# Attention with a soft mixture of experts: the second layer and the outputs in four pieces of 128 columns, with two batches to an output tile

## Chip, core and metric

One core of one Trainium2 chip (trn2). The metric is device time in microseconds (us) of one execution. TensorE is PE in the profile (PEld its weight loads), VectorE DVE, ScalarE ACT, GpSimd POOL; SP is the queue from which all transfers named here are issued. L922 is line 922 of the kernel before. In the changed kernel the same operations have other line numbers, given where they are needed.

## What is computed

```python
q_rot, k_rot = rotate(q), rotate(k)              # 8 batches, 8 heads, 576 tokens, 64 columns
attn = softmax(q_rot @ k_rot.T / sqrt(64)) ; x = attn @ v      # x: 4608 tokens x 512
logits = x @ phi                                 # 4608 x 32: 8 experts with 4 slots each
d = softmax of logits over the tokens ; slot_input = d.T @ x   # 32 x 512
for e in range(8):
    h = max(slot_input[e] @ w1[e], 0)            # 4 x 1024, w1[e]: 512 x 1024
    slot_out[e] = h @ w2[e]                      # 4 x 512,  w2[e]: 1024 x 512
c = softmax of logits over the slots
out = c @ slot_out                               # 4608 x 512
```

All inputs and outputs are float32.

## The kernel before

The attention takes some 420 us of the span and is the same in both kernels. The change lies in the last 65 us, and in one place at 424 us.

**Last pair of heads.** `natural_last` (L430) transposes the last pair's result on PE, nine transposes of 64 columns into two PSUM banks: five from the upper 64 rows, then four from the lower 64. ACT copies the first bank (L439), DVE the second (L440). `logits_add` (L454) then uses them.

**First layer.** `ffn1_steps` multiplies 32-column stationary blocks (the slots) by the 32 weight tiles of w1, 512 columns at a time (L899). DVE applies the maximum with zero (L904), `ffn1_turn` transposes the result on PE (L911) and ACT copies it to `hts` (L912).

**Weights.** w1 and w2 come in 64 tiles of 512 KB (`load_w`, L632), all issued from SP. The tiles of w2 for the output columns 0 to 255 (`mh` = 0) come first, then those for the columns 256 to 511 (`mh` = 1). The pool `wp` has 28 buffers named `w_exp`; weight tiles, small intermediate tiles and output tiles all go through it.

**Second layer.** `ffn2_steps(mh, so)` has 16 steps. A step is four matmuls with 32 stationary columns each, side by side in the four column blocks of the array, and 256 moving columns of a w2 tile (L922). Each float32 matmul shows as two rows in the trace, so a step is 8 rows. After step 15 ACT copies the sum (L926) and DVE takes the remainder (L927); `gather` adds both over the experts with two float32r matmuls (L933), and ACT copies the result to `dn` or `sl` (L936).

**Output.** `combine(mh, sl, b)` makes one output tile of 128 x 1024: for each of two blocks of 128 output columns, a matmul over 512 tokens of batch `b` (L944), a copy from PSUM by ACT for the first block and by DVE for the second (L946), and one transfer of 512 KB (L947). Batch number 8 (`crt`) stands for the 64 last tokens of all batches together. There are 9 tiles for each `mh`, 18 in all.

**Turned combine weights.** The matmul at L944 needs the softmax over the slots, transposed to `cst[q]`, one tile for two batches, and `crt`. `c_split` (L564, L565) splits it into two float32r parts, `c_tr` (L578) transposes them on PE, and copies move them out of PSUM: `c_evac` (L589, L592) in whole width, or `c_evac_late` (L602, L604) per batch, ACT for the first batch of the pair and DVE for the second. So `combine` of batch 4 needs ACT's copies of `q` = 2, batch 5 those of DVE, and batches 6 and 7 those of `q` = 3.

**Order.** PE, ACT and DVE run in the order in which the code is written. Before, `c_turn(2)` stands ahead of the second layer (L975). All 16 steps of `mh` = 0 follow, with one step of `mh` = 1 behind them, then `gather`, `c_tr(3)`, and the table `GROUPS` interleaves the nine combines of `mh` = 0 with the other 15 steps: a number is a batch, a negative number that many steps. The late copies of `q` = 3 come behind the combines of batches 1 and 2. The nine combines of `mh` = 1 end the program:

```python
LEAD_STEPS = 1
GROUPS = ((0, 1, -3), (2, 3, -4), (4, 5, 6, -8), (7, "gather", 8))
```

PSUM: `ps_c` has six banks for `gather`, `c_tr` and `combine`.

Of the kernel before, what the change touches and what calls it, by code (L numbers as in the profile page):

```python
# [19 lines left out]
DM = H * D  # L20
E, SPE, FF = 8, 4, 1024
# [6 lines left out]
N_W = 28  # L28
# [121 lines left out]
def attn_softmoe(ctx, tc, qk, v, phi, w1, w2, cs, ident, sel, seg, out):  # L150
    nc = tc.nc
    P = 128

    const = ctx.enter_context(tc.tile_pool(name="const", bufs=1))
    small = ctx.enter_context(tc.tile_pool(name="small", bufs=3))
    wp = ctx.enter_context(tc.tile_pool(name="wp", bufs=N_W))
# [3 lines left out]
    late = vals.enter_context(tc.tile_pool(name="late", bufs=2))  # L160
# [215 lines left out]
    xns = {}  # L376
# [53 lines left out]
    def natural_last():  # L430
        p = NPAIR - 1
        pp = p % NP
        xts[p] = xt = late.tile([P, S], F32, name="xt", bufs=N_X)
        ts = [bank2(1), bank2(3)]
        for h, cols in enumerate((slice(0, 320), slice(320, S))):
            t = ts[h][:, 0]
            for j in range(5 - h):
                nc.tensor.transpose(t[:, 64 * j:64 * j + 64], xns[B - 1][rows[h], j, pp * P:pp * P + P], id_sb[rows[h], rows[h]])
        nc.scalar.copy(out=xt[:, 0:320], in_=ts[0][:, 0, 0:320])  # L439
        nc.vector.tensor_copy(out=xt[:, 320:S], in_=ts[1][:, 0, 0:256])  # L440
        for t in ts:
            free(t)

# [295 lines left out]
    for t, cc in ((1, 0), (1, 1), (0, 0), (0, 1)):  # L739
        c = half[cc]  # L740
# [39 lines left out]
    seg_in, seg_sb, hts = release_att()  # L780
# [39 lines left out]
    m, al, dt, xn = state["m"], state["al"], state["dt"], xns.pop(B - 1)  # L820
# [26 lines left out]
    for c in range(2):  # L847
        for j in range(4):
            nc.tensor.matmul(sh[c][32 * j:32 * j + 32], lhsT=dn[:, 32 * j:32 * j + 32],
                             rhs=xn[:, j, 256 * c:256 * c + 256], start=True, stop=True, tile_position=(0, 32 * j))  # L850
    for i in range(NP):
        nc.tensor.matmul(rp[32 * i:32 * i + 32], lhsT=dn[0:64, P + 32 * i:P + 32 * i + 32],
                         rhs=xn[0:64, 4, i * P:(i + 1) * P], start=True, stop=True, tile_position=(0, 32 * i))
# [6 lines left out]
                            in1=e.unsqueeze(1).broadcast_to([P, NP, NS]), op=ALU.mult)  # L860
# [24 lines left out]
    for _ in range(N_LEAD):  # L885
# [22 lines left out]
    def ffn1_turn(f, hs):  # L908
        t = ps_t.tile([P, 512], F32, name="t_ps")
        for i in range(4):  # L910
            nc.tensor.transpose(t[:, i * P:(i + 1) * P], hs[:, i * P:(i + 1) * P], id_sb)  # L911
        nc.scalar.copy(out=hts[:, 192 * f:192 * f + 192].rearrange("p (b g k) -> p b g k", g=3, k=SPE)[:, :, 0:3:2],  # L912
                       in_=t.rearrange("p (b g k) -> p b g k", g=8, k=SPE)[:, :, 0:2])

    def ffn2_steps(mh, so):
        op = ps_a.tile([P, 512], F32, name="o_ps")
        og = op[:, 0:256]
        for k in range(16):
            fh, grp, f = k // 8, k // 4 % 2, k % 4
            for x in range(4):  # L920
                at = 192 * fh + 12 * (4 * f + x) + SPE * grp
                nc.tensor.matmul(og[32 * x:32 * x + 32, :], lhsT=hts[:, at:at + 32],  # L922
                                 rhs=w_tiles[4 * E + 16 * mh + 8 * fh + 4 * grp + x][:, f, :],
                                 start=(k == 0), stop=(k == 15), tile_position=(0, 32 * x))
            if k == 15:
                nc.scalar.copy(out=so[:, 0, 0, :], in_=og)  # L926
                nc.vector.tensor_tensor(out=so[:, 1, 0, :], in0=og, in1=so[:, 0, 0, :], op=ALU.subtract)  # L927
            yield

    def gather(mh, so):  # L930
        rp = ps_t.tile([P, 512], F32, name="c_ps")
# [7 lines left out]
    def combine(mh, sl, b):
        ob = wp.tile([P, 4, 256], F32, name="w_exp", bufs=N_W)  # L940
        for jj in range(2):
            o = ps_t.tile([P, 512], F32, name="c_ps")
            tokens = cst[b // 2][:, b % 2] if b < B else crt
            nc.tensor.matmul(o, lhsT=sl[:, P * jj:P * jj + P], rhs=tokens.rearrange("p j i -> p (j i)"), start=True, stop=True)  # L944
            ob2 = ob.rearrange("p j m -> p (j m)")
            (nc.vector.tensor_copy if jj else nc.scalar.copy)(out=ob2[:, 512 * jj:512 * jj + 512], in_=o)  # L946
        nc.sync.dma_start(out=out[mh, b], in_=ob2)  # L947

    turned, split = 2, 3

    def c_turns(n):
        nonlocal turned, split
        for _ in range(n):
            if turned < NP:
                c_turn(turned)
                turned += 1
            if split < min(turned + N_CS, NP):
                c_split(split)
                split += 1
# [17 lines left out]
    steps = ffn2_steps(0, sos[0])
    for k in range(16):
        next(steps)
        if k == 1:  # L980
            ffn1_turn(1, hs)
        if k == 8:
            inner.close()
            ps_s = None
            ps_t = ctx.enter_context(tc.tile_pool(name="ps_c", bufs=6, space=PSUM, reuse_waits="tile"))
    steps = ffn2_steps(1, sos[1])
    for _ in range(LEAD_STEPS):
        next(steps)
    sl0 = gather(0, sos[0])
    c_tr(turned)  # L990
    late_evac = c_evac_late(turned)
    for run_of in GROUPS:
        for b in run_of:
            if isinstance(b, str):
                sl1 = gather(1, sos[1])
            elif b < 0:
                for _ in range(-b):
                    next(steps, None)
            else:
                combine(0, sl0, b)  # L1000
                if b:
                    next(late_evac, None)
    for b in range(B + 1):
        combine(1, sl1, b)


# [50 lines left out]
```

## Time and profile before

| | us |
|---|---|
| median of 3 runs (490.79 to 492.67) | 491.97 |
| the profiled execution | 489.32 |
| its span, on which all times below lie | 487.5 |
| PE busy in the span | 455.4 |
| DVE, ACT, POOL busy | 371.7, 291.1, 288.3 |

The granted TensorE clock was 0.981 of full speed over the span, full from early on until 475 us. The profiled execution is 2.65 us below the median of the runs, and 1.8 us of it lie outside the span. The page's first part gives the busy shares; for this change the last 65 us matter, and there the stretches of the DMA engines are read beside the order of PE.

### The profile page before, as it was taken

What the parts mean: (1) busy time and instruction counts of PE and PEld (TensorE: products, weight loads), DVE (VectorE), ACT (ScalarE), POOL (GpSimd) and SP (SyncE); (2) the same over time, 40 slices, a digit from 0 to 9 for tenths busy, and PEclk for the clock granted to TensorE, in tenths of its full rate; (3) what the DMA queues carried; (4) which work ended last, traced back from release to release, by engine and by line L of the source; (5) the groups of instructions that cost most, each with busy time, mean ns of one, the idle gap of its engine ahead of it and who ended that gap; (6) DMA issues with size and microseconds to landing.
All of it is one profiled execution on the core that took longest, in us unless ns stands there. A gap on an engine that the chain in (4) does not pass through costs nothing.

```text
span 487.5 us, 23593 instructions
## 1 busy us (share of the span) xinstructions
PE 455.4 (93%) x10473; PEld 369.0 (76%) x10473; DVE 371.7 (76%) x626; ACT 291.1 (60%) x668; POOL 288.3 (59%) x320
## 2 busy tenths in 40 slices
PE   4499999999989999999999999999999999899990
PEld 2277788878878888878887888788889888844750
DVE  4999988787868897988898889888977854244370
ACT  2156766775766577657765776567657756542360
POOL 2887759909782969487948795878669102230000
PEclk9699999999999999999999999999999999999996
DMA  7258545563554355435544553354460344989887
GB/s 271 101 186 293 189 134 200 170 229 130 199 170 171 144 182 188 167 110 203 185 156 129 195 190 137 104 209 138 165 216 15 112 161 161 335 289 400 325 342 311
DMA packets 29509, 93.98 MB, mean 193 GB/s; under 512 B 5088, under 2 KB 6880, under 8 KB 29408
## 3 DMA queue, kind: packets, MB, share of 16 engines
q1 hardware_dynamic: 29388, 92.48, 53.0%
q8 instruction: 82, 1.34, 1.1%
q14 instruction: 19, 0.16, 0.1%
q10 hardware_dynamic: 20, 0.00, 0.0%
HBM read 82.95 MB, written 9.44 MB: 190 GB/s over the span
## 4 chain that ended last, share of the span: by engine, by line
PE 84%; DVE 5%; DMA 3%; ACT 2%; issue 2%; POOL 1%; SPq 1%; DVEq 0%; ACTq 0%; POOLq 0%
PE s_ps L356 32%; PE s_ps L321 25%; PE s_ps L268 7%; PE s_ps L336 3%; PE o_ps L922 3%; PE o_ps L899 3%; PE s_ps L465 2%; DMA x_in<-in_qk 2%; PE s_ps L428 2%; DVE nm L270 2%; POOL x_in L220 1%; PE s_ps L277 1%; PE s_ps L525 1%; PE c_ps L944 1%; DVE hl L233 1%
## 5 line engine op out<-in xcount | busy, mean ns | idle before, releaser
L220 POOL TENSOR_TENSOR x_in<-x_in,cs_sb 128x288 f32<-128x288 f32 x248 | 233.0, 975 | 86.5 <-DMA x_in<-in_qk 68.5
L270 DVE TENSOR_REDUCE nm<-s_ps 128x2 f32<-128x576 f32 x256 | 187.9, 752 | 53.6 <-PE s_ps L268 51.9
L322 ACT ACTIVATE a_t<-s_ps 128x576 f32<-128x576 f32 x256 | 145.9, 657 | 7.4 <-PE s_ps L321 7.3
L356 PEld LDWEIGHTS s_ps<-v_in,a_t 128*64 128x64 f32 x4608 | 138.9, 137 | 11.9 <-issue 4.4
L356 PE MATMUL s_ps<-v_in,a_t 128*64 128x66 f32 x4608 | 145.1, 222 | 1.1 <-issue 0.9
L321 PE MATMUL s_ps<-hl 64*128 64x288 f16 x1536 | 133.5, 283 | 1.0 <-DVE nm L270 0.7
L321 PEld LDWEIGHTS <-hl 64*128 64x128 f16 x1536 | 79.5, 94 | 19.9 <-issue 9.8
L321 PE MATMUL s_ps<-peak,lift 64*128 64x288 f16 x512 | 75.3, 282 | 0.5 <-issue 0.5
L268 PE MATMUL s_ps<-hl 64*128 64x288 f16 x512 | 66.4, 287 | 7.1 <-DVE nm L270 3.5
L386 ACT COPY o_sb<-s_ps 128x528 f32<-128x528 f32 x31 | 18.6, 601 | 76.2 <-PE s_ps L356 69.9
L404 POOL TENSOR_TENSOR xn<-o_sb,rr 128x640 f32<-128x640 f32 x31 | 41.1, 1333 | 31.1 <-PE s_ps L525 14.2
L229 ACT CAST hl<-x_in 128x576 f16<-128x576 f32 (+1 forms) x66 | 41.0, 656 | 25.0 <-DVE x_in L224 24.4
L233 DVE TENSOR_TENSOR hl<-x_in,hl 128x1152 f16<-128x1152 f32 x32 | 52.8, 1651 | 2.0 <-ACT hl L229 2.0
L224 DVE TENSOR_TENSOR x_in<-x_in 128x1152 f32<-128x1152 f32 (+2 forms) x36 | 48.3, 1344 | 1.0 <-POOL x_in L220 0.7
L268 PEld LDWEIGHTS <-hl 64*128 64x128 f16 x512 | 30.0, 94 | 22.4 <-issue 11.2
L321 PEld LDWEIGHTS <-lift 64*128 64x128 f16 x512 | 27.1, 94 | 5.0 <-issue 0.7
L356 PE MATMUL s_ps<-v_in,a_tr 64*64 64x66 f32 x1152 | 26.0, 224 | 0.0
L356 PEld LDWEIGHTS s_ps<-v_in,a_tr 64*64 64x64 f32 x1152 | 21.5, 133 | 4.9 <-issue 4.2
L279 DVE TENSOR_REDUCE nm<-s_ps 128x2 f32<-128x576 f32 x32 | 23.9, 749 | 1.0 <-PE s_ps L277 0.8
L336 PE MATMUL s_ps<-hl 64*64 64x320 f16 (+1 forms) x384 | 22.9, 287 | 0.5 <-DVE nm L270 0.3
L340 ACT ACTIVATE a_tr<-s_ps 128x512 f32<-128x512 f32 x32 | 19.1, 597 | 1.1 <-PE s_ps L336 0.4
L448 ACT COPY xt<-s_ps 128x576 f32<-128x576 f32 x31 | 19.0, 652 | 0.0
(170 smaller groups left out, 399.9 us busy)
## 6 DMA issues: line engine op xcount, KB each, us to landing
x_in<-in_qk SPq DMA_DIRECT2D x62, 576.0 KB
w_exp<-in_w SPq DMA_DIRECT2D x55, 512.0 KB
v_in<-in_v SPq DMA_DIRECT2D x32, 330.0 KB
out<-w_exp SPq DMA_DIRECT2D x18, 512.0 KB
wt<-in_w SPq DMA_DIRECT2D x9, 512.0 KB
peak<-mr SPq DMA_DIRECT2D x126, 0.5 KB
x_in<-in_qk SPq DMA_DIRECT2D x4, 288.0 KB
cs_sb<-in_cs SPq DMA_DIRECT2D x2, 288.0 KB
```

The source lines that it names most:

```text
L220: eng.tensor_tensor(out=x[:, :, c], in0=x[:, :, c], in1=cs_sb[:, :, c], op=ALU.mult)
L224: nc.vector.tensor_tensor(out=x[:, t, 0, c], in0=x[:, t, 0, c], in1=x[:, t, 1, c], op=ALU.add)
L229: nc.scalar.copy(out=halves[p][:, 1 + t, c], in_=loaded[p][:, t, 0, c])
L233: nc.vector.tensor_tensor(out=hl[:, 0:4:3], in0=x[:, :, 0], in1=hl[:, 1:3], op=ALU.subtract)
L268: nc.tensor.matmul(s[c, h, 0:HC], lhsT=hl[rows[h], QH, P * j + c.start:P * j + c.stop], rhs=hl[rows[h], KH, half[n]], start=True, stop=True)
L270: nc.vector.tensor_reduce(out=nm[:, n, j:8:4], in_=s[:, :, 0:HC], axis=AX.X, op=ALU.max, negate=True)
L279: nc.vector.tensor_reduce(out=nm[:, :, 8], in_=s[:, :, 0:HC], axis=AX.X, op=ALU.max, negate=True)
L321: nc.tensor.matmul(s[c, h, 0:HC], lhsT=lhs, rhs=rhs, start=(x == 0), stop=(x == 3))
L322: nc.scalar.activation(out=ats[p, b][:, :, half[n]], in_=s[:, :, 0:HC], func=AF.Exp, scale=SCALE)
L336: nc.tensor.matmul(s[rows[h ^ n], n, 0:w] if n else s[rows[h], 0, 512 - w:512], lhsT=lhs, rhs=rhs, start=(x == 0), stop=(x == 3))
L356: nc.tensor.matmul(o[rows[c], h, VW * u:VW * u + VW], lhsT=lhs, rhs=v, start=(i == 0 and u == 0), stop=(left_av[p] == 0 and u == 3 + (c == ...
L404: eng.tensor_tensor(out=xn, in0=t[:, :, :, 0:64], in1=rr.unsqueeze(3).broadcast_to([P, 2, 5, 64]), op=ALU.mult)
```

## The change

- The second layer has four passes (`p` = 0 to 3) of 16 steps with 128 moving columns instead of two with 256. Both passes of an `mh` use the same weight tiles, each half of the columns.
- `gather` and the copies around it run once for each pass, with 128 columns.
- `combine(p, b)` makes one block of 128 output columns for one batch: one matmul, one copy (ACT where `b + p` is even, else DVE). Two neighbouring batches share an output tile and one transfer of 512 KB. The rest (batch 8) is written in four transfers of 256 KB. There are 20 output transfers with the same bytes as 18 before.
- `c_turn(2)` ahead of the second layer is gone; `c_split(3)` stands there. `c_tr(2)` follows the 16 steps of piece 0, and both late turns (`q` = 2 and 3) lie between the combines of piece 0.
- `PIECES` gives the order: `(p, n)` is n steps of pass p, a number is a combine of the current piece, "g1" the gather of pass 1, "c2" `c_tr(2)`, and "e2" one half of the late copies of `q` = 2 (first ACT's, then DVE's).
- `natural_last` issues its nine transposes in turn between the two halves, and DVE's copy stands ahead of ACT's.
- The layout of the output array changes with it.

```diff
-LEAD_STEPS = 1
-GROUPS = ((0, 1, -3), (2, 3, -4), (4, 5, 6, -8), (7, "gather", 8))
+PIECES = (
+    ((0, 16), "c2", (1, 2), "g0", (1, 2), 0, 1, "e2", 2, 3, "e2", "c3", 4, 5, "e3", (1, 1), "e3", 6, 7, 8),
+    ((1, 11), (2, 3), "g1", (2, 2), 0, 1, 2, 3, 4, 5, 6, 7, 8),
+    ((2, 11), (3, 3), "g2", (3, 2), 0, 1, 2, 3, 4, 5),
+    ((3, 11), 6, "g3", 7, 8),
+    (0, 1, 2, 3, 4, 5, 6, 7, 8),
+)
...
-        for h, cols in enumerate((slice(0, 320), slice(320, S))):
-            t = ts[h][:, 0]
-            for j in range(5 - h):
-                nc.tensor.transpose(t[:, 64 * j:64 * j + 64], xns[B - 1][rows[h], j, pp * P:pp * P + P], id_sb[rows[h], rows[h]])
+        for j in range(5):
+            for h in range(2 if j < 4 else 1):
+                nc.tensor.transpose(ts[h][:, 0, 64 * j:64 * j + 64], xns[B - 1][rows[h], j, pp * P:pp * P + P],
+                                    id_sb[rows[h], rows[h]])
+        nc.vector.tensor_copy(out=xt[:, 320:S], in_=ts[1][:, 0, 0:256])
         nc.scalar.copy(out=xt[:, 0:320], in_=ts[0][:, 0, 0:320])
-        nc.vector.tensor_copy(out=xt[:, 320:S], in_=ts[1][:, 0, 0:256])
...
-    def ffn2_steps(mh, so):
+    def ffn2_steps(p, so):
         op = ps_a.tile([P, 512], F32, name="o_ps")
-        og = op[:, 0:256]
+        og = op[:, 0:P]
+        mh, cols = p // 2, slice(P * (p % 2), P * (p % 2) + P)
...
-                                 rhs=w_tiles[4 * E + 16 * mh + 8 * fh + 4 * grp + x][:, f, :],
+                                 rhs=w_tiles[4 * E + 16 * mh + 8 * fh + 4 * grp + x][:, f, cols],
...
+    def combine(p, b):
+        key, half_of = ((p, b // 2), b % 2) if b < B else (("rest", p // 2), p % 2)
+        if key not in obs:
+            obs[key] = wp.tile([P, 4, 256], F32, name="w_exp", bufs=N_W).rearrange("p j m -> p (j m)")
+        ob = obs[key][:, 512 * half_of:512 * half_of + 512]
+        o = ps_t.tile([P, 512], F32, name="c_ps")
+        tokens = cst[b // 2][:, b % 2] if b < B else crt
+        nc.tensor.matmul(o, lhsT=sls["p", p], rhs=tokens.rearrange("p j i -> p (j i)"), start=True, stop=True)
+        (nc.vector.tensor_copy if (b + p) % 2 else nc.scalar.copy)(out=ob, in_=o)
+        if b == B:
+            nc.sync.dma_start(out=out[16 + p // 2][:, 512 * half_of:512 * half_of + 512], in_=ob)
+        elif half_of:
+            nc.sync.dma_start(out=out[4 * p + b // 2], in_=obs.pop(key))
...
-    c_turns(1)
-    sos = [wp.tile([P, 2, 2, 256], F32R, name="w_exp", bufs=N_W) for _ in range(2)]
+    c_split(3)
+    sos = wp.tile([P, 4, 2, P], F32R, name="w_exp", bufs=N_W)
```

How the instructions move is shown at two places. The first is ACT from the sum of the first pass (`w_exp<-o_ps`) on. Before (L946 is the output copy, L602 and L604 the late copies of a turn):

```order
L926 CAST w_exp<-o_ps 128x256
L936 CAST dn<-c_ps 128x256
L946 COPY w_exp<-c_ps 128x512 x2
L602 CAST w_exp<-c_ps 64x2x128 x2
L604 CAST crt<-c_ps 64x64
L602 CAST w_exp<-c_ps 64x2x128 x2
L604 CAST crt<-c_ps 64x64
L946 COPY w_exp<-c_ps 128x512 x5
```

And in the changed kernel (L959 is the output copy, L607 and L609 the late copies):

```order
L932 CAST w_exp<-o_ps 128x128
L947 CAST dn<-c_ps 128x128
L959 COPY w_exp<-c_ps 128x512
L607 CAST w_exp<-c_ps 64x2x128 x2
L609 CAST crt<-c_ps 64x64
L607 CAST w_exp<-c_ps 64x2x128 x2
L609 CAST crt<-c_ps 64x64
L959 COPY w_exp<-c_ps 128x512 x2
L607 CAST w_exp<-c_ps 64x2x128 x2
L609 CAST crt<-c_ps 64x64
L607 CAST w_exp<-c_ps 64x2x128 x2
L609 CAST crt<-c_ps 64x64
```

Two groups of late copies stand among the first output copies instead of one. DVE has the same pattern, one group behind two output copies and the other behind one more.

The second place is PE from the first combines to the end. Before (L922 a step's matmul, four to a step; L944 combine, L933 gather):

```order
L944 MATMUL c_ps<-w_exp,dn 128x512 x4
L922 MATMUL o_ps<-w_exp,hts 32x256 x12
L944 MATMUL c_ps<-w_exp,dn 128x512 x4
L922 MATMUL o_ps<-w_exp,hts 32x256 x16
L944 MATMUL c_ps<-w_exp,dn 128x512 x6
L922 MATMUL o_ps<-w_exp,hts 32x256 x32
L944 MATMUL c_ps<-w_exp,dn 128x512 x2
L933 MATMUL c_ps<-w_exp,seg_sb 128x256 x2
L944 MATMUL c_ps<-crt,dn 128x512 x2
L944 MATMUL c_ps<-w_exp,sl 128x512 x16
```

In the changed kernel, from the last 12 matmuls of the steps ahead of the second gather (L928 a step's matmul, L958 combine, L941 gather):

```order
L928 MATMUL o_ps<-w_exp,hts 32x128 x12
L941 MATMUL c_ps<-w_exp,seg_sb 128x128 x2
L928 MATMUL o_ps<-w_exp,hts 32x128 x8
L958 MATMUL c_ps<-w_exp,dn 128x512 x8
L958 MATMUL c_ps<-crt,dn 128x512
L928 MATMUL o_ps<-w_exp,hts 32x128 x56
L941 MATMUL c_ps<-w_exp,seg_sb 128x128 x2
L928 MATMUL o_ps<-w_exp,hts 32x128 x8
L958 MATMUL c_ps<-w_exp,sl 128x512 x6
L928 MATMUL o_ps<-w_exp,hts 32x128 x44
```

Between the combines of one piece and those of the next now lie 16 steps (or 11) of the narrower form, with a gather among them.

## Rows read from the trace of the kernel before

**Rows 1.** Stretches: busy us (instructions) by engine, TensorE clock, DMA share, GB/s.

```profile
441.00:456.00 15.00, 14.87 (x197) 9.45 (x189) 4.29 (x11) 3.21 (x9) 0.87 (x1) 1.00 1.02 411
456.00:459.40 3.40, 3.39 (x36) 2.12 (x35) 1.43 (x3) 2.17 (x6) 0.00 (x0) 1.00 0.28 110
459.40:463.20 3.80, 3.80 (x47) 2.12 (x40) 2.73 (x8) 2.19 (x7) 0.00 (x0) 1.00 1.01 406
463.20:465.10 1.90, 1.90 (x24) 1.10 (x26) 1.90 (x4) 1.50 (x3) 0.00 (x0) 1.00 0.07 22
465.10:484.50 19.40, 9.34 (x76) 5.24 (x68) 7.75 (x13) 6.43 (x13) 0.00 (x0) 0.86 1.01 404
484.50:487.50 3.00, 0.00 (x0) 0.00 (x0) 0.00 (x0) 0.00 (x0) 0.00 (x0) 0.50 0.04 15
```

**Rows 2.** Transfers issued from SP, and the page's issue line: start, us, count; KB.

```profile
458.57 22.61 SPq L947 DMA_DIRECT2D out<-w_exp  x18
out<-w_exp SPq DMA_DIRECT2D x18, 512.0 KB
```

**Rows 3.** Chain that ended last, in order of time: start, us, what.

```profile
443.03 3.57 PE o_ps L899 x32
449.00 6.70 PE o_ps L922 x120
470.45 2.92 DMA out<-w_exp
```

**Rows 4.** Timeline of PE between the first combines: start, us, instructions.

```profile
459.60 1.20 PE L944 MATMUL c_ps<-w_exp,dn 128*128 128x512 f32 x4
460.73 1.93 PE L922 MATMUL o_ps<-w_exp,hts 128*32 128x256 f32 x32
462.60 1.67 PE L944 MATMUL c_ps<-w_exp,dn 128*128 128x512 f32 x6
464.20 3.66 PE L922 MATMUL o_ps<-w_exp,hts 128*32 128x256 f32 x64
467.79 0.73 PE L944 MATMUL c_ps<-w_exp,dn 128*128 128x512 f32 x2
```

**Rows 5.** Line L454 and what follows on PE: the nearest narrow matmuls.

```profile
L454 PE MATMUL s_ps<-xt,phi_sb x48: 219/246/297, 424.7 to 425.7; 128*32 128x128 f32 x24, 128*32 128x64 f32 x24
...
424.75 1.20 PE L454 MATMUL s_ps<-xt,phi_sb 128*32 128x128 f32 x48
...
425.87 0.88 PE L578 MATMUL sp_ps<-id_sb,csp 128*128 128x128 f32 x6
```

**Rows 6.** Timeline of ACT and DVE: output copies (L946) and late turn copies (L602).

```profile
457.58 1.07 ACT L946 COPY w_exp<-c_ps 128x512 f32<-128x512 f32 x2 [0.59 <-PE c_ps L944]
457.82 1.29 DVE L946 COPY w_exp<-c_ps 128x512 f32<-128x512 f32 x2 [1.68 <-PE c_ps L944]
458.54 0.75 ACT L602 CAST w_exp<-c_ps 64x256 fp32r<-64x256 f32 x2
...
460.51 1.07 ACT L946 COPY w_exp<-c_ps 128x512 f32<-128x512 f32 x2
...
460.98 0.84 DVE L602 CAST w_exp<-c_ps 64x256 fp32r<-64x256 f32 x2
...
463.19 2.48 DVE L946 COPY w_exp<-c_ps 128x512 f32<-128x512 f32 x4
```

**Rows 7.** Groups by shape: copy of 128 columns, and gather of 256 columns.

```profile
L933 PE MATMUL c_ps<-w_exp,seg_sb 128*128 128x256 f32 x4 | 1.5, 377 | 0.2
...
L912 ACT COPY hts<-t_ps 128x128 f32<-128x128 f32 x2 | 0.5, 262 | 4.7 <-PE t_ps L911 4.7
```

**Rows 8.** PE at 424 us, the page's instruction queue, and the attention's busiest PE line.

```profile
424.17 0.52 PE L438 MATMUL s_ps<-id_sb,xn 64*128 64x64 f32 x9 [1.19 <-ACT xt L448]
...
q8 instruction: 82, 1.34, 1.1%
...
L356 PE MATMUL s_ps<-v_in,a_t 128*64 128x66 f32 x4608 | 145.1, 222 | 1.1 <-issue 0.9
```

More of the change, by code (lines that the diff above doesn't have):

```diff
@@ L922, in ffn2_steps @@
                 nc.tensor.matmul(og[32 * x:32 * x + 32, :], lhsT=hts[:, at:at + 32],
-                                 rhs=w_tiles[4 * E + 16 * mh + 8 * fh + 4 * grp + x][:, f, :],
+                                 rhs=w_tiles[4 * E + 16 * mh + 8 * fh + 4 * grp + x][:, f, cols],
                                  start=(k == 0), stop=(k == 15), tile_position=(0, 32 * x))
             if k == 15:
-                nc.scalar.copy(out=so[:, 0, 0, :], in_=og)
-                nc.vector.tensor_tensor(out=so[:, 1, 0, :], in0=og, in1=so[:, 0, 0, :], op=ALU.subtract)
+                nc.scalar.copy(out=so[:, 0], in_=og)
@@ L928, in ffn2_steps, with gather @@
+                nc.vector.tensor_tensor(out=so[:, 1], in0=og, in1=so[:, 0], op=ALU.subtract)
             yield
-    def gather(mh, so):
+    sls = {}
+    def gather(p, so):
         rp = ps_t.tile([P, 512], F32, name="c_ps")
         for a in range(2):
-            nc.tensor.matmul(rp[:, 0:256], lhsT=seg_sb[:, 64 - 64 * a:192 - 64 * a], rhs=so[:, a, 0, :],
+            nc.tensor.matmul(rp[:, 0:P], lhsT=seg_sb[:, 64 - 64 * a:192 - 64 * a], rhs=so[:, a],
                              start=(a == 0), stop=(a == 1))
-        sl = tail.tile([P, 256], F32R, name="sl") if mh else small.tile([P, 2 * P], F32R, name="dn", bufs=1)
-        nc.scalar.copy(out=sl, in_=rp[:, 0:256])
-        return sl
@@ L939, in combine @@
[L939 to L959, printed above, removed]
+        if p % 2 == 0:
+            sls[p // 2] = (tail.tile([P, 2 * P], F32R, name="sl") if p else
+                           small.tile([P, 2 * P], F32R, name="dn", bufs=1))
+        sls["p", p] = sl = sls[p // 2][:, P * (p % 2):P * (p % 2) + P]
@@ new lines, in gather @@
+        nc.scalar.copy(out=sl, in_=rp[:, 0:P])
+    obs = {}
+    def combine(p, b):
[11 more added lines that the diff above has]
+            nc.sync.dma_start(out=out[4 * p + b // 2], in_=obs.pop(key))
@@ L974, in attn_softmoe, with advance @@
     hs = next(second)
-    c_turns(1)
-    sos = [wp.tile([P, 2, 2, 256], F32R, name="w_exp", bufs=N_W) for _ in range(2)]
[L977 to L998, printed above, removed]
-            else:
[L1000 to L1004, printed above, removed]
+    c_split(3)
+    sos = wp.tile([P, 4, 2, P], F32R, name="w_exp", bufs=N_W)
+    steps = {}
+    late = {}
+    def advance(p, n):
+        nonlocal ps_s, ps_t
+        if p not in steps:
+            steps[p] = ffn2_steps(p, sos[:, p])
+        for k in range(n):
+            next(steps[p])
+            if p == 0 and k == 1:
+                ffn1_turn(1, hs)
+            if p == 0 and k == 8:
+                inner.close()
+                ps_s = None
+                ps_t = ctx.enter_context(tc.tile_pool(name="ps_c", bufs=6, space=PSUM, reuse_waits="tile"))
+    piece = 0
+    for run_of in PIECES:
+        for x in run_of:
+            if isinstance(x, tuple):
+                advance(*x)
+            elif isinstance(x, int):
+                combine(piece, x)
+                if x == B:
+                    piece += 1
+            elif x[0] == "g":
+                gather(int(x[1]), sos[:, int(x[1])])
+            elif x[0] == "c":
+                c_tr(int(x[1]))
+                late[x[1]] = c_evac_late(int(x[1]))
+            else:
+                next(late[x[1]])
 def kernel(q, k, v, moe_phi, moe_w1, moe_w2):
@@ L1048 @@
         args.append(nc.dram_tensor(f"in_{name}", a.shape, mybir.dt.from_np(a.dtype), kind="ExternalInput").ap())
-    args.append(nc.dram_tensor("out_0", (2, B + 1, 128, 1024), F32, kind="ExternalOutput").ap())
+    args.append(nc.dram_tensor("out_0", (18, 128, 1024), F32, kind="ExternalOutput").ap())
     with tile_mod.TileContext(nc) as tc:
@@ L1052 @@
     r = run_bass_kernel_spmd(nc, [arrays], core_ids=[0])
-    o = r.results[0]["out_0"].reshape(2, B + 1, 128, 2, 512)
-    main = o[:, :B].reshape(2, B, 128, 2, 4, 2, 64).transpose(1, 5, 4, 6, 0, 3, 2).reshape(B, 2, 256, DM)
-    rest = o[:, B].reshape(2, 128, 2, B, 64).transpose(3, 4, 0, 2, 1).reshape(B, 64, DM)
+    o = r.results[0]["out_0"].reshape(18, 128, 2, 512)
+    o, rest = o[:16].reshape(2, 2, 4, 128, 2, 512).transpose(0, 2, 4, 3, 1, 5).reshape(2, B, 128, 2, 512), o[16:]
+    main = o.reshape(2, B, 128, 2, 4, 2, 64).transpose(1, 5, 4, 6, 0, 3, 2).reshape(B, 2, 256, DM)
+    rest = rest.reshape(2, 128, 2, B, 64).transpose(3, 4, 0, 2, 1).reshape(B, 64, DM)
     return np.concatenate([main[:, 0], rest, main[:, 1]], axis=1).reshape(B * S, DM)
```

## Prediction

> **What bounds the kernel now.** I read the windows table first, because the end of this kernel is a stretch of transfers. From 441 to 456 us the DMA engines are full with the weights of w2 (share 1.02, 411 GB/s); then two holes follow, and from 465.1 to 484.5 they are full again with outputs, until the span ends 3.0 us later [rows 1]. The holes are worth 0.72 x 3.4 = 2.4 us (456 to 459.4) and 0.93 x 1.9 = 1.8 us (463.2 to 465.1), together **4.2 us**: the most that a better order of the same transfers can gain. The bytes are fixed: the 18 outputs of 512 KB are issued from 458.57 us on [rows 2], three go between the holes and 15 in the last 19.4 us, so one takes 1.29 us. The first data moves 0.83 us after the first issue (459.4 against 458.57).
>
> Next the chain: it runs through PE (first layer to 446.6, steps from 449.0 to 455.7) and only at the end over an output transfer [rows 3]. So the holes exist because PE delivers outputs too late: none before 458.57, and a second shortage after the first combines, where eight steps (464.20 to 467.79) stand ahead of the next [rows 4]. A change of order helps only if PE and the copies behind it feed the queue without a new shortage.
>
> **Unit costs.** Steps of 256 columns: eight take 3.59 us and four 1.87 [rows 4], so one is 1.72 / 4 = 0.43, and each stint of steps costs 0.15 beside that. Combines: six take 1.60 and four 1.13, so one is 0.235 and a stint adds 0.19.
>
> A step of 128 columns is not in this trace. Half of 0.43 is 0.215. From above: the 24 four-block matmuls of 128 columns and 24 of 64 columns at L454 (12 groups of four rows) end when the next operation starts, 1.12 us after their start [rows 5]; by columns two thirds of that, 0.75, fall to six groups of 128 columns, 0.125 for each, and a step is two groups: 0.25. I take 0.22, nearer the half, because the L454 span also holds a start. The 64 narrow steps cost 14.1 us where 32 wide ones cost 13.8: **+0.3 us** (at 0.25, +2.2). By the changed order there are ten step stints where there were about five, at 0.34 for a pair of stints: +1.7 us on PE. Both count only where PE is what the transfers wait for.
>
> By a rule of the Trainium skill ("TensorE: Matmul & The Clock Gate", section "Back-to-back issue gap") pairs of weight load and matmul sustain about 81 ns per matmul at 128 columns, and by that a step of eight would be 0.65 us. No row shows that pace for four column blocks side by side: rows 5 have 24 + 24 in 1.12 us, 23 ns each.
>
> Copies: an ACT output copy follows the last by 1.07 − 0.59 = 0.48 us and lasts 0.59; DVE 1.29 − 0.69 = 0.60 and 0.69. The late group of turned weights keeps ACT from 458.54 to 460.51, **1.97 us**, and DVE from 460.98 to 463.19, **2.21 us** [rows 6]. The gather with 128 columns is not shown: it lies between half of the 256-column one (two of 377 ns [rows 7], which overlap) and nearly no saving, so four instead of two cost 0 to +0.7 us; I take 0.2, and 0.26 for the copy behind it [rows 7]. Two transfers of 256 KB for one of 512 KB: the same bytes, 0 to +0.2; I take 0.
>
> `natural_last`: nine transposes take 0.52 us [rows 8]. In turn between the halves they may overlap, and the two copies start in another order: 0 to −0.3; I take −0.1.
>
> **The new order, step by step.**
> *Start of piece 0.* PE is free at 446.6. 16 narrow steps are 3.5, a stint 0.15, the turn of the first layer 0.6 and its wait for the maximum 0.4: 451.3. `c_tr(2)`, six transposes (0.88 with the last one's latency [rows 5]), 0.8: 452.1. Two steps, gather, two steps: 453.7. Combines 0 and 1, 0.66, and a copy of 0.69 behind: the first output is issued at **455.0**, 3.5 us earlier than now. The weights then last until about 456.7 (the 0.28 x 3.4 us of work after 456 close up), so the hole of 2.4 us is gone.
>
> *Rest of piece 0.* Now the late copies stand in the way. ACT copies block 0, then its late group of `q` = 2 until 456.5, then blocks 2 and 4; output 1 is issued at 457.1. DVE copies blocks 1 and 3 by 455.5, then its late group, 2.2: 457.7, and combine 5 can only then be done and copied: output 2 at 458.7, data 459.5 (hole 0.2). The second pair of late groups: ACT 457.6 to 459.5, DVE 458.6 to 460.8, so combine 7 waits for 460.8, and output 3 is issued at 461.7, data 462.6 after the queue emptied at 460.8: **hole 1.8**. PE, first in line behind each of these waits, stands idle for some 4 us at combines 4 to 7, and the 14 steps that piece 1 still needs are queued behind them.
>
> *Piece 1.* PE gets to it at 461.3: 14 steps 3.1, two stints of steps 0.3, gather 0.2, two more steps 0.4, two combines 0.66, a copy 0.69: 466.6, data 467.4. The queue finished output 3 and the rest's 256 KB at 464.5: **hole 2.9**.
>
> *Pieces 2 and 3.* A piece costs PE 16 x 0.22 + 9 x 0.235 + 0.34 + gather and its change of form 0.4 = 6.4 us; its 4.5 transfers last 5.8. So piece 2 begins at 473.0, data 473.9, after the queue ended at 473.3: hole 0.6. Its fourth output stands behind 11 steps and a gather: issued about 477.7, data 478.5, after three transfers from 473.9 ended at 477.7: hole 0.8. From there six transfers' worth of bytes remain, 7.8: the bulk ends at 486.3, against 484.5 [rows 1].
>
> *Sum.* Holes 0.2 + 1.8 + 2.9 + 0.6 + 0.8 = 6.3 where there were 4.2. End of the bulk +1.8; the last 3.0 us, partly engines that lag the others, may shrink since the late holes let them catch up: −0.2 (0 to −1); `natural_last` −0.1. **+1.5 us**: the profiled execution goes from 489.3 to 490.8, and the median of the runs, 2.65 us above it, from 491.97 to **493.5**. A measurement can tell about 0.5% of this kernel, 2.46 us, from no change.
>
> **Rivals.**
> *A, the late copies do not hold PE.* If the copies slip between the combines, the 4 us at combines 4 to 7 go; piece 1 arrives that much sooner, the holes of 1.8 and 2.9 shrink to under 1 together, and 2.2 remain of 6.3: 4.2 − 2.2 = −2.0, about 490. For it: PE has the steps of piece 1 to do. Against: in the written order only one step lies between combines 5 and 6, and both groups are as long as rows 6 show. Chance 0.15.
>
> *B, the queue never empties.* −4.2: 487.8. It needs A, and pieces of under 5.8 us on PE: steps of 0.18. Chance 0.08.
>
> *C, PE's instructions arrive too late.* The instruction queue moves 1.34 MB in 82 packets [rows 8], so code is fetched during the run; and PE stood 1.19 us before L438 [rows 8], of which the copy that the row names may be only a part. The narrow steps use it twice as fast as now (eight rows in 0.22 us where it was 0.43). Price: about 1.1 us for each stall, one to five in the four passes, on top of the forecast; the bound of 2.46 is passed from the first (1.5 + 1.1). With steps at 0.25 it ends likewise: about 495.5. Against: L356 ran 4608 narrow rows with 1.1 us idle before them in all, of which 0.9 for issue [rows 8]. Chance 0.22, 494.6 to 499.
>
> *D, a narrow step costs as much as a wide one.* Then the piece takes PE 64 x 0.21 = 13.4 us longer in all, all of it with an empty queue: about 507. Rows 5 speak against. Chance 0.03.
>
> *E, single-file pairs.* If the four blocks no longer ran side by side, a step would be eight passes in a row; at the 219 ns latency of rows 5 not even overlapped it were 1.75 us, and at a pace of three times 0.22 the 64 steps cost 42 us in place of 14: about 520. The skill's rule above would give this size. Rows 5 disagree. Chance 0.02.
>
> **How the numbers follow.** The forecast has 0.50. Faster by over 0.5% (below 489.5) is B: 0.08. Within 0.5% are the forecast and A: 0.65. Slower (above 494.4) are C, D, E: 0.27. The range leaves out B, D, E and the upper end of C: 490.0 (A) to 497.0 (three stalls: 493.5 + 3.3).
>
> **What would show it.** Right: the first output issued near 455.0; no hole at 456 to 459; holes at about 461 to 462.6 and 464.5 to 467.4; PE idle some 4 us at combines 4 to 7, released by ACT and DVE copies; late groups of some 2 us each on both engines, twice; 6.4 us from piece to piece; a step at 0.22; the granted clock full up to the last combines. Wrong: outputs that run through from 456 (A or B), PE idle with nothing awaited (C), a step of more than 0.25, or a first output later than 456, which would mean that the turn at the start of piece 0 costs more than it saves.

## Result and profile after

The changed kernel took 497.87 us (median of 6 runs, 495.39 to 503.07) where the kernel before took 491.75 (6 runs): ratio 1.0116, interval 1.0087 to 1.0144, so some 5.7 us slower. The ratio leaves out one slow run, that of 503.07 us. The forecast was +1.5 us and 493.5, with a range up to 497.0.

The two profiled executions have spans of 487.5 and 495.4 us. To see where the 7.9 us lie, I read both from three common points. The first transpose of `natural_last` starts at 424.17 before [rows 8] and at 428.05 after; the first layer ends on PE at 446.60 [rows 3] and at 450.43. So 3.9 us come ahead of `natural_last`, where the two programs are the same, and nothing from there to the end of the first layer (22.4 us both). The rest is the **tail**, from the end of the first layer to the end of the span: 487.5 − 446.6 = 40.9 us before, 495.4 − 450.4 = 45.0 after, **+4.1 us**.

The stretches of that tail in the changed kernel (columns as in [rows 1]):

```profile
450.43:459.90 9.47, 8.78 (x183) 6.66 (x174) 2.57 (x5) 2.58 (x8) 0.62 (x1) 1.00 1.02 405
459.90:465.10 5.20, 2.52 (x12) 1.17 (x13) 4.45 (x13) 4.07 (x12) 0.00 (x0) 0.84 0.82 336
465.10:467.00 1.90, 1.90 (x26) 1.24 (x29) 0.69 (x1) 0.58 (x1) 0.00 (x0) 0.50 0.08 35
467.00:469.45 2.45, 2.45 (x52) 2.20 (x48) 0.00 (x0) 0.00 (x0) 0.00 (x0) 0.50 0.84 322
469.45:474.35 4.90, 4.90 (x77) 3.74 (x67) 1.98 (x4) 1.99 (x6) 0.00 (x0) 0.92 0.02 5
474.35:480.20 5.85, 5.85 (x137) 4.74 (x136) 2.51 (x6) 2.19 (x7) 0.00 (x0) 1.00 1.01 394
480.20:481.00 0.80, 0.80 (x31) 0.80 (x33) 0.80 (x2) 0.50 (x2) 0.00 (x0) 1.00 0.22 87
485.70:492.10 6.40, 0.94 (x4) 0.44 (x3) 2.15 (x4) 1.37 (x3) 0.00 (x0) 0.89 1.01 399
492.10:495.40 3.30, 0.00 (x0) 0.00 (x0) 0.00 (x0) 0.00 (x0) 0.00 (x0) 0.50 0.47 185
```

The hole of 2.4 us behind the weights is gone, as forecast: the DMA share stays near 1 to 459.9. But between 469.45 and 474.35 the queue is empty for **4.8 us** (0.98 x 4.9). And the clock, 1.00 around the first combines of the kernel before [rows 1], falls in 459.9 to 465.1 and is 0.50 until past 469.45. The timeline of PE in these stretches (L958 combine, L928 step, L941 gather) shows why and what it cost:

```profile
460.55 0.49 PE L958 MATMUL c_ps<-w_exp,dn 128*128 128x512 f32 x1 [0.89 <-ACT crt L609]
461.52 0.50 PE L958 MATMUL c_ps<-w_exp,dn 128*128 128x512 f32 x1 [0.48 <-DVE w_exp L607]
...
463.33 0.74 PE L958 MATMUL c_ps<-w_exp,dn 128*128 128x512 f32 x1 [0.95 <-ACT w_exp L607]
464.67 0.80 PE L958 MATMUL c_ps<-w_exp,dn 128*128 128x512 f32 x1 [0.60 <-DVE w_exp L607]
465.26 0.63 PE L958 MATMUL c_ps<-crt,dn 128*128 128x512 f32 x1
465.82 3.21 PE L928 MATMUL o_ps<-wt,hts 128*32 128x128 f32 x56
468.81 2.41 PE L928 MATMUL o_ps<-w_exp,hts 128*32 128x128 f32 x56
471.15 0.47 PE L941 MATMUL c_ps<-w_exp,seg_sb 128*128 128x128 f32 x2
472.12 2.13 PE L958 MATMUL c_ps<-w_exp,dn 128*128 128x512 f32 x8
```

PE waits four times for the late copies, ahead of combines 4, 5, 6 and 7, together 2.9 us where the forecast had some 4. Combines 6 and 7 take 0.74 and 0.80 us in place of 0.49, and the 14 steps of piece 1 (112 rows) last from 465.82 to 471.15, **5.33 us**; the same 14 steps of piece 2 last 3.20 (474.45 to 477.65). The granted clock is 0.50 for most of the former and 1.00 for the latter: 1.2 GHz in place of 2.4. The late copies themselves are as long as forecast: ACT 458.56 to 460.52 = 1.96 us.

```profile
458.56 0.75 ACT L607 CAST w_exp<-c_ps 64x256 fp32r<-64x256 f32 x2
...
460.52 1.15 ACT L959 COPY w_exp<-c_ps 128x512 f32<-128x512 f32 x2
```

Outputs issued from SP, the first group of each piece:

```profile
459.06 7.85 SPq L963 DMA_DIRECT2D out<-w_exp  x4
...
473.50 2.89 SPq L963 DMA_DIRECT2D out<-w_exp  x4
...
480.13 5.13 SPq L963 DMA_DIRECT2D out<-w_exp  x4
```

Counted from the end of the first layer, the pieces begin at 8.6, 23.1 and 29.7 us. The forecast, counted likewise, had 8.4, 20.0 and 26.4.

### The profile page after: what moved, and what is told of

It reads as the page before. It is cut to its first block, busy times and chain, and to the rows that moved or that the text cites. A ratio compares the mean times of both kernels' runs of the same rounds, so it can differ in the third digit from the quotient of the medians.

```text
span 495.4 us, 24131 instructions
## 1 busy us (share of the span) xinstructions
PE 461.6 (93%) x10733; PEld 375.4 (76%) x10733; DVE 377.8 (76%) x631; ACT 292.3 (59%) x675; POOL 284.7 (57%) x320
## 4 chain that ended last, share of the span: by engine, by line
PE 77%; DVE 10%; DMA 5%; ACT 3%; issue 2%; SPq 1%; POOL 1%; DVEq 0%; ACTq 0%; POOLq 0%
PE s_ps L361 28%; PE s_ps L326 22%; PE s_ps L273 6%; DMA x_in<-in_qk 4%; PE o_ps L928 3%; PE s_ps L341 3%; DVE nm L275 3%; PE o_ps L904 3%; DVE x_in L229 2%; DVE hl L238 2%; PE s_ps L470 2%; ACT a_t L327 2%; PE s_ps L433 2%; PE c_ps L958 1%; DMA v_in<-in_v 1%
## 5 line engine op out<-in xcount | busy, mean ns | idle before, releaser
L409 POOL TENSOR_TENSOR xn<-o_sb,rr 128x640 f32<-128x640 f32 x31 | 41.0, 1329 | 31.1 <-PE s_ps L530 14.2
L238 DVE TENSOR_TENSOR hl<-x_in,hl 128x1152 f16<-128x1152 f32 x32 | 55.4, 1731 | 2.0 <-ACT hl L234 2.0
L234 ACT CAST hl<-x_in 128x576 f16<-128x576 f32 (+1 forms) x66 | 41.0, 657 | 26.4 <-DVE x_in L229 26.3
L229 DVE TENSOR_TENSOR x_in<-x_in 128x1152 f32<-128x1152 f32 (+2 forms) x36 | 50.3, 1398 | 0.1
L273 PEld LDWEIGHTS <-hl 64*128 64x128 f16 x512 | 29.7, 95 | 22.1 <-issue 9.8
```

Of the source, the lines that this page charges most:

```text
L229: nc.vector.tensor_tensor(out=x[:, t, 0, c], in0=x[:, t, 0, c], in1=x[:, t, 1, c], op=ALU.add)
L234: nc.scalar.copy(out=halves[p][:, 1 + t, c], in_=loaded[p][:, t, 0, c])
L238: nc.vector.tensor_tensor(out=hl[:, 0:4:3], in0=x[:, :, 0], in1=hl[:, 1:3], op=ALU.subtract)
L273: nc.tensor.matmul(s[c, h, 0:HC], lhsT=hl[rows[h], QH, P * j + c.start:P * j + c.stop], rhs=hl[rows[h], KH, half[n]], start=True, stop=True)
L409: eng.tensor_tensor(out=xn, in0=t[:, :, :, 0:64], in1=rr.unsqueeze(3).broadcast_to([P, 2, 5, 64]), op=ALU.mult)
```

## Experiments

The theory: PE's waits behind the late copies let the clock fall, and the work of piece 1 that stands behind them ran at half speed. Its rivals: the waits alone, the narrow steps, `natural_last`, or something ahead of the tail. All tails count from the end of the first layer; ratios are to the kernel before, run on the same chip. A tail is that of one profiled execution, a ratio that of several, and versions measured in one session share the runs of the kernel before.

| kernel | ratio (interval) | tail, us | first output of piece 1, us |
|---|---|---|---|
| the change | 1.0116 (1.0087 to 1.0144) | 45.0 | 23.1 |
| the change again | 1.0084 (1.0047 to 1.0122) | 44.2 | 22.0 |
| old `natural_last` in it | 1.0105 (1.0051 to 1.0159) | 44.8 | 22.7 |
| spin behind the waits | 1.0115 (1.0065 to 1.0165) | 43.8 | 21.6 |
| spin in the waits | 1.0041 (1.0016 to 1.0065) | 43.0 | 20.8 |
| steps in the waits | 1.0016 (0.9981 to 1.0051) | 40.9 | 18.7 |
| turn of `q` = 2 ahead | 1.0035 (0.9995 to 1.0075) | 40.5 | 18.4 |
| no late copies | 1.0010 (0.9976 to 1.0044) | 39.4 | 17.5 |
| turn of `q` = 3 behind combine 1, old `natural_last` | 0.9976 (0.9944 to 1.0009) | 38.6 | 16.4 |
| the same, new `natural_last` | 0.9966 (0.9941 to 0.9992) | 38.7 | 16.4 |
| before, new `natural_last` | 0.9973 (0.9938 to 1.0008) | 40.9 | |
| before, against itself | 1.0020 (0.9990 to 1.0050) | 40.7 | |

**The clock alone.** Extra steps, whose results nothing uses, stand in PE's waits. First try:

```diff
         tokens = cst[b // 2][:, b % 2] if b < B else crt
+        if p == 0 and 4 <= b < 8:
+            for k in range(3):
+                for x in range(4):
+                    nc.tensor.matmul(o[32 * x:32 * x + 32, 0:P], lhsT=hts[:, 32 * k:32 * k + 32],
+                                     rhs=w_tiles[4 * E + x][:, k, 0:P], start=True, stop=True, tile_position=(0, 32 * x))
```

> The changed kernel with three extra narrow steps (0.65 us, results overwritten) ahead of each of combines 4 to 7 of piece 0, in the time that TensorE waits there. Measure: from the end of the first layer on TensorE to the end of the span, 40.9 us before, 45.0 in the changed kernel. Theory 1 (the wait let the granted clock fall to 0.50, and the next 10 steps of piece 1 ran at half speed): clock 1.00 from 462 to 472 us, the 112 rows of piece 1 in 3.0 us in place of 5.1, so 42.9 us. Theory 2 (the wait alone makes the loss, the clock is a side effect that costs nothing since transfers are awaited): 45.0 or, with the extra steps in the way, 45.5.

The clock stayed at 1.00 around the combines and the 14 steps took 3.19 us, but the tail fell by 1.2 us only, to 43.8, between what the two theories gave, and the ratio did not fall (1.0115). The first extra steps (L961) waited as long as combine 4 does in the changed kernel:

```profile
465.15 0.31 PE L961 MATMUL c_ps<-w_exp,hts 128*32 128x128 f32 x3 [0.89 <-ACT crt L609]
```

They read none of the turned weights and write only the bank of combine 4. So the wait there is one for that bank too, and not only for the turned weights as the prediction had it. The extra steps stood behind the wait and not in it; combine 4 came 0.8 us later, and the fourth output 0.75. The second try writes to columns of the running sum's bank that nothing uses:

```diff
-    ((0, 16), "c2", (1, 2), "g0", (1, 2), 0, 1, "e2", 2, 3, "e2", "c3", 4, 5, "e3", (1, 1), "e3", 6, 7, 8),
+    ((0, 16), "c2", (1, 2), "g0", (1, 2), 0, 1, "e2", 2, 3, "e2", "c3", "s", 4, "s", 5, "e3", (1, 1), "s", "e3", 6, "s", 7, 8),
...
+    def spin():
+        for k in range(3):
+            for x in range(4):
+                nc.tensor.matmul(tops[1][32 * x:32 * x + 32, 3 * P:4 * P], lhsT=hts[:, 32 * k:32 * k + 32],
+                                 rhs=w_tiles[4 * E + x][:, k, 0:P], start=False, stop=False, tile_position=(0, 32 * x))
```

> The changed kernel with the same three extra narrow steps in the waits of combines 4 to 7, but writing to unused columns of the sum's own bank, so that they wait for nothing and stand in the wait itself (in the first try they waited for the combine's bank and came behind the wait). Theory 1 (clock): outputs of piece 0 as in the changed kernel (8.6, 10.7, 12.4, 16.1 less some 0.3 for combines at full clock), clock 1.00 throughout, the 14 steps of piece 1 in 3.2 us in place of 5.3, measure 45.0 - 2.1 - 0.3 = 42.6 us, which is what the prediction gave without the clock; ratio 1.004. Theory 2 (waits alone): 45.0 us, 1.008.

PE of that kernel from combine 7 to the gather (L966 combine, L949 gather), and its stretches from combine 4 on:

```profile
462.24 0.50 PE L966 MATMUL c_ps<-w_exp,dn 128*128 128x512 f32 x1 [0.28 <-DVE w_exp L607]
462.98 1.74 PE L928 MATMUL o_ps<-wt,hts 128*32 128x128 f32 x56
464.54 1.71 PE L928 MATMUL o_ps<-w_exp,hts 128*32 128x128 f32 x56
466.18 0.45 PE L949 MATMUL c_ps<-w_exp,seg_sb 128*128 128x128 f32 x2
```

```profile
456.75:459.75 3.00, 2.90 (x61) 1.79 (x62) 2.32 (x8) 2.92 (x9) 0.00 (x0) 1.00 0.68 279
459.75:463.75 4.00, 3.66 (x87) 2.51 (x83) 3.29 (x8) 2.22 (x6) 0.00 (x0) 1.00 0.56 218
463.75:467.75 4.00, 4.00 (x113) 3.44 (x106) 0.37 (x2) 0.53 (x2) 0.00 (x0) 1.00 0.53 202
```

The order of the real work is that of the changed kernel, the copies are the same, and the outputs of piece 0 leave at nearly the same times (8.6, 10.7, 12.7, 16.1 against 8.6, 10.7, 12.4, 16.1). What differs is the clock: 1.00, the 14 steps in 3.20 us, the tail 43.0 us (expected 42.6) and the ratio 1.0041. The clock is worth 2.0 us of the 4.1; the other 2.1 us remain with the clock kept, and are the waits and holes for which the forecast had +1.6.

**The change twice more.** First unchanged, then with the old `natural_last`:

> The changed kernel once more, for a second profile and more times beside the kernel before. If the tail is fixed by the program and the rest is chance: measure from the first layer's end to the end 45.0 us within 0.3, clock 0.50 for some 7 us from combine 6 or 7 on, attention ending anywhere between 423 and 431 us, ratio 1.0083 (4.1 us of 491.5) in the mean. If something outside the tail costs too: ratio 1.011 again.

> The changed kernel with natural_last as before. Measure 45.0 us as in the changed kernel, and the clock falls to 0.50 at about 463 us again. Theory A (natural_last costs 1.8 us): ratio 1.0083 (4.1 us of 490.7). Theory B (natural_last costs nothing): ratio 1.0116 as measured for the whole change, or anything between as chance has it.

In both the clock fell to 0.50 again between combines 5 and 8. It came back earlier in the first: the 14 steps took 4.27 us there (464.56 to 468.83), between 3.20 and 5.33, and the tail is 44.2 us, between 43.0 and 45.0.

```profile
463.41 0.80 PE L958 MATMUL c_ps<-w_exp,dn 128*128 128x512 f32 x1 [0.82 <-DVE w_exp L607]
464.56 2.81 PE L928 MATMUL o_ps<-wt,hts 128*32 128x128 f32 x56
467.20 1.70 PE L928 MATMUL o_ps<-w_exp,hts 128*32 128x128 f32 x56
468.83 0.46 PE L941 MATMUL c_ps<-w_exp,seg_sb 128*128 128x128 f32 x2
```

Its ratio is 1.0084, of which the tail (+3.3 us) gives 0.67%; in the other two some 0.3% lie outside the tail.

**Real work in the waits.**

```diff
-    ... 0, 1, "e2", 2, 3, "e2", "c3", 4, 5, "e3", (1, 1), "e3", 6, 7, 8),
-    ((1, 11), (2, 3), "g1", ...
+    ... 0, 1, "e2", 2, 3, "e2", "c3", (1, 3), 4, (1, 3), 5, "e3", (1, 1), "e3", (1, 2), 6, (1, 2), 7, 8),
+    ((1, 1), (2, 3), "g1", ...
```

> The changed kernel with 10 steps of piece 1 moved from behind combine 8 into the waits of combines 4 to 7. Theory 1 (clock): TensorE keeps 1.00, the steps cost nothing in the waits; first output of piece 1 is issued 2.1 (clock) + 10 x 0.22 = 4.3 us earlier, the measure (end of first layer to end of span) goes from 45.0 to about 41. Theory 2 (only the order counts): 2.2 us earlier, 42.8 us.

```profile
460.00:463.00 3.00, 2.62 (x55) 1.58 (x51) 2.33 (x8) 2.90 (x9) 0.00 (x0) 1.00 0.76 309
463.00:466.00 3.00, 2.50 (x47) 1.62 (x51) 2.37 (x6) 1.34 (x4) 0.00 (x0) 1.00 0.47 182
466.00:470.00 4.00, 4.00 (x55) 2.77 (x47) 2.39 (x5) 2.28 (x6) 0.00 (x0) 1.00 0.61 244
```

Clock 1.00, tail 40.9, 4.1 us less. Of these 2.0 are the clock's by the spin; the other 2.1 fit the ten steps, which now cost no time of their own (10 x 0.22). This alone brings the change back to the time before, within the interval.

**Where the turns stand.**

```diff
+    c_turn(2)
     c_split(3)
...
-    ((0, 16), "c2", (1, 2), "g0", (1, 2), 0, 1, "e2", 2, 3, "e2", "c3", 4, 5, "e3", (1, 1), "e3", 6, 7, 8),
+    ((0, 16), "c3", (1, 2), "g0", (1, 2), 0, 1, "e3", 2, 3, "e3", 4, 5, (1, 1), 6, 7, 8),
```

> The changed kernel with the turn of q = 2 back ahead of the second layer, as before, so that only one late group (q = 3) stands among the combines. If two late groups are what makes TensorE wait: idle at combines 4 to 7 under 1.5 us, clock 1.00 throughout, hole after piece 0 under 1.5 us, measure 40 to 41 us (45.0 now). If the narrow steps or the many stints are the loss, the measure stays above 43.

The tail is 40.5: with one late turn among the combines PE waits 0.64 and 0.48 us, ahead of combines 6 and 7, and is busy for 4.88 of 6 us there; the clock holds. The hole behind piece 0 is 1.8 us (share 0.24 from 470.0 to 472.4), longer than the 1.5 expected. In the tail, the pieces of 128 columns with many stints are no loss by themselves.

```profile
462.00:468.00 6.00, 4.88 (x91) 3.14 (x93) 4.60 (x10) 4.27 (x11) 0.00 (x0) 1.00 0.69 277
```

With both turns ahead of the combines (`c_turn(2)` as above, `c_turn(3)` behind step 5 of piece 0, no "c" and "e" entries):

> Both turns (q = 2 and 3) done before the combines, with the copies in the time of the first 16 steps, no late copies at all. If late copies are all that holds the outputs: no hole in the transfers until the end, 23.3 us of outputs behind the weights, measure 40.9 - 4.2 = 36.7 us, time about 4 us below the kernel before. If a piece at 6.4 us of TensorE against 5.8 us of transfers is the next bound: holes of 0.6 at each piece, measure 38 us. If the attention is really slower by 3 us in the changed code, the time is still only about equal to before.

The tail is 39.4, not 36.7 to 38. The first output is issued 10.9 us after the first layer. The copies of a turn in this form run one after the other: DVE's group waits for the end of ACT's (L594 and L597 are the copies), and PE waits for them at the next turn (L583) and, behind that turn's copies, at the gather (L941).

```profile
450.41 1.17 ACT L594 CAST w_exp<-sp_ps 64x512 fp32r<-64x512 f32 x2 [2.87 <-PE sp_ps L583]
...
451.88 1.39 DVE L594 CAST w_exp<-sp_ps 64x512 fp32r<-64x512 f32 x2 [1.56 <-ACT crt L597]
...
453.72 0.85 PE L583 MATMUL sp_ps<-id_sb,csp 128*128 128x128 f32 x6 [0.45 <-DVE crt L597]
...
458.15 0.33 PE L941 MATMUL c_ps<-w_exp,seg_sb 128*128 128x128 f32 x1 [0.55 <-DVE w_exp L933]
```

So the last version keeps the turn of `q` = 3 behind combine 1, with its late copies behind those of blocks 0 to 5 and steps of pieces 1 and 2 in the wait; once with the old `natural_last` and once with the new:

```diff
+    c_turn(2)
     c_split(3)
...
+    ((0, 16), (1, 2), "g0", (1, 2), 0, 1, "c3", 2, 3, 4, 5, "e3", "e3", (1, 12), 6, (2, 2), 7, 8),
+    ("g1", (2, 2), 0, 1, 2, 3, 4, 5, 6, 7, 8),
+    ((2, 12), (3, 3), "g2", (3, 2), 0, 1, 2, 3, 4, 5),
```

> A version meant to beat both: natural_last as before, turn of q = 2 ahead of the second layer, turn of q = 3 behind combines 0 and 1 with its late copies behind the copies of blocks 0 to 5, and all 12 left steps of piece 1 in the wait for them; two steps of pass 2 between combines 6 and 7. By theory 1 (clock and waits): clock 1.00 until the last combines, first output issued 8.9 us after the first layer's end, hole after piece 0 under 1 us, holes of 0.6 to 0.8 at each piece since TensorE needs 6.4 us for one and the transfers 5.8; measure 37.5 to 38 us, 3 us under before, ratio 0.994. If the turn ahead of the second layer delays the first output as it did in the run without late copies (10.9 us), measure 39.4 and ratio 0.998.

> The change with its turns mended alone: turn of q = 2 ahead of the second layer, that of q = 3 behind combine 1, as in the version with the old natural_last, here with the new one. Measure 38.6 us as there, clock 1.00 until the last combines; ratio 0.995 if nothing outside the tail differs, 0.998 if the 1 to 2 us outside the tail are real.

Tails 38.6 and 38.7 (expected 37.5 to 38, with a hole of under 1 us), ratios 0.9976 and 0.9966. It beats the changed kernel clearly. Of the kernel before it is 1.7 us ahead by the second ratio, whose interval ends at 0.9992; as that kernel against itself came out at 1.0020, this is likely and not shown. Its stretches (new `natural_last`) hold one hole of 1.6 us (0.80 x 2.0), and after it the queue is at 0.96 for 19.8 us; the clock falls only once the last combines are done:

```profile
459.00:463.50 4.50, 4.50 (x117) 3.65 (x117) 3.45 (x10) 3.22 (x10) 0.00 (x0) 1.00 0.91 358
463.50:465.50 2.00, 1.90 (x24) 1.38 (x23) 1.12 (x2) 1.03 (x3) 0.00 (x0) 1.00 0.20 74
465.50:485.30 19.80, 13.68 (x252) 10.37 (x250) 8.72 (x16) 7.61 (x17) 0.00 (x0) 0.96 0.96 378
```

**What lies outside the tail.** The new order of `natural_last` (as in the diff of the change) alone on the kernel before, the kernel before for a second profile, and the kernel before against itself:

> The kernel before with only the new order of natural_last (nine transposes in turn, DVE's copy ahead of ACT's). Question: the changed kernel and the four runs so far are each some 1 to 3 us (mean near 1.8) slower in their medians than their measure from the first layer's end to the end of the span explains. Theory A: natural_last does that: ratio 1.003 to 1.004, first nine transposes or what follows them later by over 1 us. Theory B (chance of the executions, or the code's place): ratio 1.000 within 0.3%, measure 40.9 us as before, transposes within 0.3 us of the 22.4 us to the end of the first layer.

> The kernel before once more, for a second profile of it: where its time varies. If executions differ by the attention, the first of the nine transposes of natural_last starts at another time than 424.2 us (up to 431 in the runs so far), while the measure from the first layer's end to the end stays at 40.9 us within 0.3.

> The kernel before against itself: ratio 1.000. How far it comes out from 1 says what these comparisons can tell; the two profiles of it so far have the same 40.8 to 40.9 us from the first layer's end and differ by 6.2 us ahead of natural_last.

`natural_last` costs nothing that can be seen: ratio 0.9973, its nine transposes 0.47 us in place of 0.52, 22.4 us to the end of the first layer. The kernel before differs from itself: in its second profile (496.46 us) the tail is 40.8 again, but `natural_last` starts at 430.42, 6.2 us later than in the first [rows 8]; in its third, the one against itself (493.74 us), it starts at 427.50, and the tail is 40.7. What PE waited for in the attention of the second (26 to 422 us), the largest entries:

```profile
PE s_ps L356 <- DMA v_in<-in_v: 3.2, 3, 2.3
PE s_ps L356 <- issue: 1.5, 2, 1.1
```

In the first one the largest was 0.9, for issue. And behind the wait ahead of `natural_last`, 1.75 us where the first had 1.19, the clock fell there too:

```profile
430.42 0.52 PE L438 MATMUL s_ps<-id_sb,xn 64*128 64x64 f32 x9 [1.75 <-issue]
```

```profile
428.42:430.42 2.00, 0.25 (x16) 0.23 (x5) 0.50 (x3) 0.75 (x2) 0.04 (x1) 1.00 0.97 371
430.42:432.42 2.00, 2.00 (x62) 1.76 (x62) 0.46 (x2) 0.68 (x3) 0.00 (x0) 0.88 1.00 401
432.42:434.42 2.00, 2.00 (x12) 1.84 (x13) 0.53 (x2) 1.14 (x6) 0.49 (x2) 0.50 0.60 203
```

From there to the end of the first layer it took 23.4 us, 1.0 more. So the 3.9 us by which the two profiles differ ahead of the tail are within what one kernel does from execution to execution. The clock fell at this place in 6 of the 14 profiled executions, in two of the three of the kernel before, and cost 1.0 to 1.3 us each time. The length of the wait alone doesn't decide it: behind 2.02 us in the change again the clock held, behind 2.01 in the spin in the waits it fell.

## Why the prediction was wrong

- **The failed step** is piece 1: "PE gets to it at 461.3: 14 steps 3.1". They took 5.3 us, because the clock was not what the prediction took it to be, "the granted clock full up to the last combines". I had worked out that PE would stand idle for some 4 us at combines 4 to 7 (2.9 by the trace), and priced that wait as lost time alone. No rival had the clock in it, though [rows 1] show 0.50 once PE has nothing to do. The spin in the waits gives the size: 45.0 − 43.0 = 2.0 us.
- The Trainium skill has a rule that points this way ("TensorE: Matmul & The Clock Gate", section "HAM oscillation — how this bites in real kernels"): where TensorE waits between blocks of matmuls, the next block can start at half the clock, again and again. The trace agrees in kind: 0.50 from 465.1 to 469.45. The rule tells of waits for transfers of several us, though, and the four waits here are of 0.48 to 0.95 us, so it would have raised the question and not answered it.
- **Without the clock the sum was near.** Forecast for the tail +1.6 (+1.5 with the −0.1 of `natural_last`), 42.5 us; measured with the clock kept, 43.0, with the first output of piece 1 at 20.8 where I had 20.0. First output 8.4 against 8.6, second 10.5 against 10.7, third 12.1 against 12.4, combine 7 at 14.2 against 14.2; the fourth output at 15.1 against 16.1, which leaves at 16.1 with the clock kept too (its combine came 0.25 us later there, behind the extra steps), so that most of this 1.0 us is not the clock's and was not in the sum: from the start of combine 7 to the issue I had 0.9 us, and it took 1.9, and 1.6 with the clock kept. A step took 0.22 us, ACT's late groups 1.96; a piece took PE 6.6 us (473.50 to 480.13) where I had 6.4.
- The holes: 2.4 us gone as forecast; 0.9 (0.18 x 5.2) between the first outputs, where I had 0.2; 1.7 (0.92 x 1.9) ahead of the fourth output, forecast with 1.8; 4.8 ahead of piece 1 where I had 2.9; 0.6 (0.78 x 0.80) ahead of piece 2, as forecast. The forecast's own holes add up to +2.1 (6.3 − 4.2) where it took +1.8 for the end of the bulk; 0.3 of it is that it let the weights last until 456.7, and 456 + 0.28 x 3.4 is 456.95.
- **The time of the whole kernel** lay outside the range also because the range was built from costs in the tail and left out that executions differ. A tail of +4.1 us is +0.83%: 495.9 us, still inside the range. The first measurement gave 1.16%, the second of the same kernel 0.84% with a tail of +3.3 us, and the kernel before against itself 0.20%. So chance is part of it. But in all ten measurements of versions with four pieces the ratio is at or above what the tail gives, by 0 to 2.7 us and 1.3 in the mean, where the two of versions with the old passes lie 1.3 below and 1.2 above. Something outside the tail may cost about 1 us; what it is stays open, and the prediction had no term for it. With the clock kept the time would have stayed inside the range all the same: 497.5 (1.0116 x 491.75) less 2.0.
- Rival C, late code in the four passes, didn't come: PE's waits behind the first layer's turn, 2.9 us, all end with copies of ACT and DVE, and none stands at L928. D and E fell with the step of 0.22. Rival A, copies that don't hold PE, did not come with this order; the last version, which moves them, gave its size: 38.7 us, −2.2, forecast with −2.0 (the prediction's "4.2 − 2.2" is to be read as 2.2 − 4.2).

## What to carry to other kernels

Waits on TensorE can have two prices: their own length, and the matmuls behind them at 1.2 in place of 2.4 GHz (here some 2 us each). Before moving work of ACT or DVE in front of a TensorE instruction, write down what TensorE does in the meantime, and put steps that are due anyhow there. Compare two profiles from a point behind which the programs differ, not by their whole spans.

## What was not expected of the hardware

- Between combines 4 and 7 the clock fell though PE worked between its waits of 0.89, 0.48, 0.95 and 0.60 us. In all three executions of this order it fell; in all three versions with extra steps or steps of piece 1 in the waits it stayed up there.
- The same program started `natural_last` at 424.2, 427.5 and 430.4 us, and its clock fell there in the last two of these executions and not in the first: 1.0 of the 7.1 us between the spans of the first and the last.
- Extra matmuls that write the bank of the next result did not fill the wait for that bank (0.89 us ahead of them, at combine 4); those in a free part of another bank did, and combine 4 started 10.1 us after the first layer there as in the changed kernel.
